# A chunked delta rule feeding an MoE layer: four weight loads wait for ScalarE, and the whole order is written anew

## The chip, the cores and the metric

The kernel runs on one NeuronCore of a Trainium2 chip. The metric is the time of one execution on the device, in microseconds; of several executions the median counts. TensorE (PE) does the matmuls, VectorE (DVE), ScalarE (ACT) and GpSimd (POOL) the work between them, and the sync engine (SP) issues most of the DMAs.

## The reference, cut to what matters

```python
def _attn_ref(q, k, v, beta):               # q, k, v: (4, 8, 768, 48) float32
    k_n = k / (np.linalg.norm(k, axis=-1, keepdims=True) + 1e-06)
    state = np.zeros((B, H, D, D), dtype=np.float32)
    for t in range(S):
        kt, vt, bt = (k_n[:, :, t], v[:, :, t], beta[:, :, t, None])
        y[:, :, t] = np.einsum('bhd,bhde->bhe', q[:, :, t], state)
        v_old = np.einsum('bhde,bhd->bhe', state, kt)
        state = state + bt[:, :, :, None] * np.einsum('bhd,bhe->bhde', kt, vt - v_old)

def _moe_ref(x, w_in, w_out):               # x: y as (3072, 384); w_in (384, 2048), w_out (2048, 384) float64
    h = x @ w_in
    sp = np.where(h > 20.0, h, np.log1p(np.exp(np.minimum(h, 20.0))))
    return (h * np.tanh(sp)) @ w_out
```

A recurrence over 768 steps, for 32 pairs of batch and head, makes y. Every row of y, with the 8 heads side by side, then goes through two matmuls with the Mish function between them.

## The kernel before

**Two halves, woven together.** The 768 steps are cut into 12 chunks of 64 (`NS`). Within a chunk the recurrence is solved as a triangular system; between chunks a 48x48 state is carried. In the program's names, chunk n goes through these stages: `pg` (products of k with k, TensorE) and `d` (masked on DVE); the solve on DVE, an alternation of `pr` and `gt` steps that each need the one before; its result `tu` and `tt`; a merge of the 16-blocks (`ma`, its copy `ym` on ScalarE, `mb`, an addition into `tt` on DVE, then `tn`); `ta` and its copies `at` on ScalarE; `tb` and its copies into `tt`; `pz`; then `py` (the chunk's y) with `ps` (the new state). y is transposed (`xt`) and split into a rounded part and a rest (`x`, ScalarE and DVE). With x the chunk's 256 rows run through the MoE: eight units `g1` (18 matmuls into `h`, then Mish to `e`, its rounded part and its rest `g`) and eight units `g2` (12 matmuls into `acc`). Solves serve two chunks at once, so that of chunks 0 and 1 stands at the very start of the kernel, and no MoE work can start before y of chunk 0 is there.

**The weights.** They come as float64, read as pairs of int32. `load_w` loads 28 tiles: twelve of w_in (`ri0` to `ri11`, 128x1024, two DMAs of 256 KB) and sixteen of w_out (`ro0` to `ro15`, 128x768, two DMAs of 192 KB). The list `parts` numbers them: ri0, ri1, ri2, ro0 to ro3, ri3 to ri5, ro4 to ro7, and so on. `convert` makes float32 of a tile in eight pieces: a clamp on DVE (L1325), a scaling on ScalarE (L1328, or L1331 with one more step on DVE), a shift on DVE (L1338), the join into `mi`, `mo` or `spare` on DVE (L1342), a rounding on ScalarE (L1346), and the rest by two matmuls (`loi`, `loo`, L1354 and L1358) and a copy on ScalarE (L1360), for later tiles by a DMA that adds. The raw tile is overwritten in the end.

**What sets the order.** Every piece of work is a step of a generator that is put on a heap with a number; `run` takes them in the order of the numbers and writes their instructions out, and the scheduler keeps that order on each engine. The numbers stand in a table, `TT`: for each generator the places of its steps, 1612 in all. A second table, `SLOT`, says which buffer a tile takes out of its pool. An instruction waits for the semaphores of what it needs, and everything behind it on its engine waits with it. `warm` matmuls on a tile of zeros are filler on TensorE; they wait for nothing but `zero`.

**DMA queues.** Loads are issued by SP, in the order of their steps; only k's second halves and beta are issued by ScalarE. The loads share eight semaphores in turn, so that a load waits until the eighth before it has landed. `half` is a 128x1 tile that GpSimd writes at the start.

Of the kernel before, what the change touches and what calls it, by code (L numbers as in the profile page):

```python
# [10 lines left out]
F32 = mybir.dt.float32  # L11
# [18 lines left out]
def bcast_in(ap, n):  # L30
# [3 lines left out]

TT = {
    'warm0.501': [0],
    'warm11.602': [1],
    'loadk0': [2],
    'turn_k(0,0)': [3],
    'loadq': [4],  # L40
    'loada': [5],
    'loadk1': [6],
    'warm0.5': [7],
    'turn_k(0,0).0>1': [8],
    'early0': [9, 31, 35, 41, 53, 58, 60, 61, 63, 67, 69, 75, 76, 78, 81, 82, 83, 85, 89, 92, 101, 106, 110, 112, 114, 122, 123, 125, 129, 131, 132, 133, 134, 135, 137, 326, 985],
# [84 lines left out]
    'scale_v(0,1)': [140],  # L130
    'warm12.3': [141],
    'merge0': [144, 146, 164, 166],
    'warm32.2': [147],
    'merge0.0>1': [148],
    'cv6': [151, 177, 199, 243, 246, 255, 259, 308, 703],
    'warm12.003': [153],
    'merge0.1>1': [154],
    'warm11.8': [155],
    'cv7': [158, 183, 214, 222, 240, 297, 313, 364, 1086],
    'loadi6': [159],  # L140
    'loado7': [160],
    'warm0.602': [161],
    'cv9': [163, 188, 231, 258, 269, 277, 289, 295, 992],
    'loadi7': [165],
    'ats_gq[0,1].0>2': [168],
    'merge0.2>1': [169],
    'cv22': [170, 182, 190, 316, 473, 476, 482, 485, 495],
    'warm11.603': [171],
    'warm27.9': [172],
    'warm11.501': [173],  # L150
    'cv17': [174, 210, 337, 402, 418, 420, 440, 441, 755],
    'cv12': [178, 195, 244, 324, 325, 333, 335, 342, 372],
    'merge0.3>1': [179],
    'ats_a[0,1]': [184],
    'warm29.501': [189],
    'cv8': [191, 226, 233, 264, 271, 274, 285, 302, 1000],
    'loado5': [192],
    'cv13': [193, 247, 273, 354, 370, 373, 375, 386, 1334],
    'ats_a[0,0]': [194],
    'cv14': [197, 296, 318, 343, 360, 363, 366, 381, 452],  # L160
    'loado15': [200],
    'ats_a[0,1].0>1': [201],
    'loado13': [202],
    'merge1': [209, 212, 268, 284],
    'ats_a[0,0].0>1': [213],
    'cv15': [215, 219, 221, 350, 358, 362, 371, 380, 1332],
    'loadi8': [218],
    'loadp': [220],
    'merge1.1>1': [223],
    'loadx': [224],  # L170
    'warm46.601': [227],
    'cv11': [228, 249, 251, 283, 286, 320, 332, 338, 881],
    'unit(1,)': [229],
    'warm8.0': [230],
    'cv25': [232, 266, 344, 382, 508, 509, 526, 529, 547],
    'merge1.0>1': [234],
    'ats_b[0,0]': [235],
    'loads': [236],
    'ats_b[0,1]': [238],
    'ats_gq[0,1].0>1': [245],  # L180
    'warm12.301': [248],
    'loadi9': [250],
    'unit(0,)': [252],
    'ats_b[0,0].0>1': [253],
    'ats_b[0,1].0>1': [256],
    'ats_z[0,0]': [257],
    'cv16': [260, 305, 334, 399, 403, 415, 419, 423, 1511],
    'ats_z[0,0].0>1': [261],
    'cv23': [262, 288, 314, 414, 480, 487, 489, 497, 504],
    'ats_z[0,1]': [265],  # L190
    'ats_z[0,1].0>1': [267],
    'merge1.2>1': [270],
    'ats_y[0,0]': [272],
    'ats_y[0,0].0>1': [275],
    'warm12.401': [276],
    'cv21': [278, 322, 330, 396, 435, 446, 461, 462, 472],
    'warm11.801': [279],
    'cv20': [280, 323, 383, 451, 453, 471, 481, 490, 1350],
    'cv27': [281, 351, 374, 530, 548, 551, 561, 566, 578],
    'ats_y[0,1]': [282],  # L200
    'turn_q(1,0)': [287],
    'loadk2': [290],
    'scale_v(1,1)': [291],
    'merge1.3>1': [292],
    'ats_y[0,1].0>1': [293],
    'turn(0,)': [294],
    'turn(0,).0>1': [298],
    'turn_q(1,1)': [299],
    'turn(0,).0>2': [300],
    'turn(0,).0>3': [301],  # L210
    'early1': [303, 353, 355, 368, 384, 390, 395, 400, 401, 404, 407, 408, 413, 416, 422, 424, 427, 428, 432, 433, 434, 445, 450, 455, 458, 460, 463, 464, 475, 478, 479, 484, 491, 494, 500, 505, 507, 510, 512, 513, 515, 518, 520, 527, 531, 532, 533, 537, 539, 540, 543, 544, 545, 546, 553, 557, 559, 560, 563, 568, 571, 572, 574, 575, 576, 577, 580, 584, 586, 588, 602, 613],
    'ats_a[1]': [304],
    'ats_a[1].0>1': [306],
    'scale_v(1,0)': [307],
    'ats_gq[1,0]': [309],
    'turn(0,).0>4': [310],
    'ats_b[1]': [315],
    'ats_gq[1,0].0>1': [317],
    'g1.0.0': [319],
    'ats_b[1].0>1': [327],  # L220
    'ats_gq[1,0].0>2': [328],
    'loadk3': [329],
    'ats_z[1,0]+s_gq[1,1]': [331],
    'warm12.001': [336],
    'ats_z[1,0]+s_gq[1,1].0>3': [339],
    'ats_z[1,0]+s_gq[1,1].0>1': [340],
    'loado14': [346],
    'g1.0.0.0>1': [347],
    'warm42.1': [348],
    'ats_z[1,0]+s_gq[1,1].0>2': [349],  # L230
    'g1.0.0.0>2': [352],
    'g1.0.0.0>3': [356],
    'cv26': [357, 417, 483, 528, 534, 550, 554, 555, 562],
    'ats_y[1,0]': [359],
    'loado12': [361],
    'cv24': [365, 387, 442, 459, 499, 506, 514, 516, 521],
    'g1.0.1': [367],
    'ats_y[1,0].0>1': [369],
    'warm11.701': [376],
    'warm12.2': [377],  # L240
    'g1.0.1.0>1': [378],
    'warm46.6': [379],
    'early1.2>1': [385],
    'early1.3>1': [388],
    'early1.4>1': [389],
    'ats_z[1,1]': [392],
    'g1.0.3': [393],
    'early1.5>1': [394],
    'early2': [397, 502, 585, 589, 493, 590, 600, 609, 616, 622, 625, 626, 628, 632, 634, 643, 644, 651, 655, 663, 664, 665, 675, 676, 678, 679, 680, 681, 682, 684, 685, 688, 690, 691, 692, 693, 694, 695, 700, 707, 708, 709, 711, 712, 715, 716, 719, 725, 727, 728, 733, 738, 739, 740, 742, 744, 745, 746, 747, 749, 752, 753, 757, 758, 760, 761, 764, 768, 770, 771, 777, 786, 798, 817],
    'g1.0.2': [398],  # L250
# [1905 lines left out]
```

## Time and profile before

| | before |
|---|---|
| median of three runs | 636.4 us (632.79 to 640.93) |
| the profiled execution | 633.69 us |
| its span, first to last instruction | 631.9 us |
| mean granted TensorE clock | 0.985 |
| TensorE busy | 605.8 us, 96% |
| DVE busy | 384.2 us, 61% |
| ScalarE busy | 287.2 us, 45% |
| GpSimd busy | 77.8 us, 12% |

A busy share is a mean over stages with different limits, and TensorE's holds filler too. What bounds a stage is read from the chain of waits: from the last instruction back, at each step, to what released it. A time in brackets behind a row of the timeline is the time for which the engine stood before it. The granted clock is a share of full speed.

### The profile page before, as it was taken

The numbers are of one execution on the slowest core, as the hardware profiler recorded it, in microseconds if no ns is written. First come the engines' busy times: TensorE is split into PE (matmuls) and PEld (weight loads), VectorE is DVE, ScalarE is ACT, GpSimd is POOL, SyncE is SP. The second block draws the span as 40 slices with busy tenths as digits, with TensorE's granted clock in tenths as the row PEclk, the third lists the DMA queues.
The fourth block names the chain that finished last, engine by engine and source line by source line (L and its number), as shares of the span: only waits on it lengthen the run. The fifth ranks groups of instructions, "written<-read, shape, count | busy, mean of one in ns | idle before, by whom it ended". The sixth has DMA issues, their size and how long they took to land.

```text
span 631.9 us, 22179 instructions
## 1 busy us (share of the span) xinstructions
PE 605.8 (96%) x9707; PEld 567.1 (90%) x9718; DVE 384.2 (61%) x837; ACT 287.2 (45%) x555; POOL 77.8 (12%) x134
## 2 busy tenths in 40 slices
PE   6888899989999998999999999999999999999997
PEld 4555789889999998999999999999999999999996
DVE  1986678899669899775568567874464321511120
ACT  2356878644543453625444435424432534333141
POOL 5100123323101040020100102210021010000000
PEclk9997989989999999999999999999999999999999
DMA  8996568921433134223223222312212132000011
GB/s 192 278 345 132 89 133 140 147 50 32 71 52 73 27 52 61 50 43 49 47 41 52 52 28 33 65 33 52 33 29 44 28 52 52 1 7 20 1 26 25
DMA packets 161807, 43.21 MB, mean 68 GB/s; under 512 B 149008, under 2 KB 157712, under 8 KB 161712
## 3 DMA queue, kind: packets, MB, share of 16 engines
q1 hardware_dynamic: 156800, 37.12, 29.7%
q0 software_dynamic: 2736, 4.20, 4.0%
q8 instruction: 76, 1.25, 0.8%
q10 hardware_dynamic: 2176, 0.49, 0.4%
q14 instruction: 19, 0.16, 0.1%
HBM read 32.87 MB, written 4.72 MB: 59 GB/s over the span
## 4 chain that ended last, share of the span: by engine, by line
PE 73%; DVE 12%; DMA 5%; SPq 5%; issue 3%; ACT 1%; DVEq 0%
PE acc L1884 27%; PE h L1850 26%; SPq L1266 5%; PE py L1659 3%; PE pz L1659 3%; PE gq L1659 3%; PE pg L1466 3%; DVE gt L1529 2%; DVE pr L1527 2%; PE ps L1659 2%; DVE g L1867 1%; DMA ri<-in_moe_w_in_dram 1%; DMA xx<-in_q_dram 1%; PE warm L1910 1%; DMA kt<-in_k_dram 1%
## 5 line engine op out<-in xcount | busy, mean ns | idle before, releaser
L1884 PE MATMUL acc<-wo,g 128*128 128x384 f32 x1152 | 218.9, 341 | 3.1 <-DVE g L1867 3.1
L1850 PE MATMUL h<-x,wi 128*128 128x256 f32 x1728 | 219.9, 283 | 1.3 <-issue 1.3
L1850 PEld LDWEIGHTS h<-x,wi 128*128 128x128 f32 x1728 | 214.4, 190 | 2.7 <-issue 1.4
L1884 PEld LDWEIGHTS acc<-wo,g 128*128 128x128 f32 x1152 | 198.1, 188 | 5.4 <-DVE g L1867 3.7
L1867 DVE TENSOR_TENSOR g<-e,g 128x512 fp32r<-128x512 f32 x96 | 66.8, 703 | 95.9 <-ACT g L1866 95.5
L1865 ACT ACTIVATE e<-h 128x512 f32<-128x512 f32 x96 | 57.1, 598 | 118.2 <-PE h L1850 81.8
L1866 ACT CAST g<-e 128x512 fp32r<-128x512 f32 x96 | 58.9, 621 | 58.6 <-PE acc L1884 54.8
L1529 DVE TENSOR_TENSOR gt<-gt,pr 128x58 f32<-128x58 f32 (+9 forms) x164 | 60.4, 369 | 4.1
L1527 DVE TENSOR_TENSOR pr<-gt 128x58 f32<-128x58 f32 (+9 forms) x164 | 58.7, 358 | 4.0
L1659 PE MATMUL gq<-xx,kt 48*64 48x112 f32 (+1 forms) x768 | 50.5, 271 | 0.6 <-PE ps L1659 0.4
L1659 PEld LDWEIGHTS pz<-vt,tt 64*64 64x64 f32 x768 | 44.1, 137 | 5.0 <-issue 2.1
L1659 PE MATMUL pz<-vt,tt 64*64 64x48 f32 x768 | 47.8, 227 | 0.8 <-DVE vt L1745 0.8
L1644 DVE STREAM_TRANSPOSE xx<-xx 128x1024 f32<-128x1024 f32 x20 | 24.9, 1244 | 38.8 <-DMA xx<-in_q_dram 30.5
L1659 PEld LDWEIGHTS gq<-xx,kt 48*64 48x64 f32 x768 | 44.8, 133 | 1.9 <-issue 0.8
L1770 ACT COPY xx<-pz 64x384 f32<-64x384 f32 x48 | 22.8, 474 | 41.1 <-PE gq L1659 19.1
L1659 PEld LDWEIGHTS py<-xx 128*64 128x64 f32 x768 | 37.6, 138 | 4.2 <-issue 1.2
L1659 PE MATMUL py<-xx 128*64 128x48 f32 x768 | 41.1, 224 | 0.0
L1748 DVE TENSOR_TENSOR xx<-gq,amask 64x256 f32<-64x256 f32 x96 | 40.2, 418 | 0.9 <-issue 0.2
L1659 PE MATMUL ps<-xx 128*48 128x48 f32 x704 | 37.6, 208 | 0.0
L1637 POOL TENSOR_TENSOR vt<-vt,ne 128x384 f32<-128x384 f32 x24 | 21.2, 891 | 126.6 <-DMA vt<-in_v_dram 126.1
L1568 POOL COPY tt<-d 32x512 f32<-32x512 f32 x40 | 26.5, 663 | 72.3 <-DVE d L1549 49.5
L1659 PEld LDWEIGHTS ps<-xx 128*48 128x48 f32 x704 | 31.4, 125 | 0.0
(138 smaller groups left out, 596.2 us busy)
## 6 DMA issues: line engine op xcount, KB each, us to landing
ri<-in_moe_w_in_dram SPq DMA_DIRECT2D x24, 256.0 KB, 5.2
ro<-in_moe_w_out_dram SPq DMA_DIRECT2D x32, 192.0 KB, 5.1
kt<-in_k_dram SPq DMA_DIRECT2D x76, 64.0 KB, 3.3
vt<-in_v_dram SPq DMA_DIRECT2D x48, 96.0 KB, 3.1
xx<-in_k_dram SPq DMA_DIRECT2D x48, 96.0 KB, 3.2
out_dram<-o SPq DMA_DIRECT2D x48, 96.0 KB, 2.2
xx<-in_q_dram SPq DMA_DIRECT2D x80, 32.0 KB, 2.4
wo<-mo POOLq DMA_DIRECT2D x9, 192.0 KB, 3.9
```

The lines of the kernel that those rows point to most:

```text
L1266: m = (nc.scalar if turns[0] else nc.sync).dma_start(out=dst, in_=src)
L1527: nc.vector.tensor_tensor(out=pv, in0=nj, in1=xj, op=ALU.mult)
L1529: nc.vector.tensor_tensor(out=below, in0=below, in1=pv, op=ALU.add)
L1568: nc.gpsimd.tensor_copy(out=tt2[r, t2, :, c0:c0 + 32], in_=dts[g][r, t2])
L1644: nc.vector.transpose(x, x)
L1659: last[:] = [nc.tensor.matmul(*a, start=True, stop=True)]
L1748: nc.vector.tensor_tensor(out=x[r, p4, hh, D:D + C], in0=ps[r, :, d:], in1=bcast_mid(amask[r], 4), op=ALU.mult)
L1850: nc.tensor.matmul(h[:, f2, :], wt["i", f * P // WI * NCH + c][:, i2, f0:f0 + P], x[:, c, :], start=(i == 0), stop=(i == 3 * NCH - 1))
L1865: for d, f in ((0.7, lambda: nc.scalar.activation(e, h, AF.Mish)), (0.7, lambda: nc.scalar.copy(out=gg[:, 0], in_=e)), (0.8, lambda: nc.ve ...
L1866: (0.7, lambda: nc.scalar.copy(out=gg[:, 0], in_=e)),
L1867: (0.8, lambda: nc.vector.tensor_tensor(out=gg[:, 1], in0=e, in1=gg[:, 0], op=ALU.subtract))):
L1884: nc.tensor.matmul(acc[t], gg[:, a, f2, ts_], wt["o", f][:, i2, :], start=(f == 0 and i == 0), stop=(f == NF - 1 and i == 2))
```

## The change

A new function `gate(k)` makes the raw tile of weight k and lets ScalarE write its first column, a copy of `half`. The load of that tile overwrites the column and so has to wait for the copy. Four weights have a gate, by their places in `parts`: ri0 (0), ro0 (3), ro3 (6) and ro4 (10). The column's value is of no use to anything.

```diff
+GATES = (0, 3, 6, 10)
 TT = {
...
+    'loadk1': [0],
...
+    'gate(0,)': [2],
...
-            r = raw[kind, i] = cp.tile([P, src.shape[1]], I32, tag=f"w{kind}{i}", name=f"r{kind}{i}")
+            if (kind, i) not in raw:
+                raw[kind, i] = cp.tile([P, src.shape[1]], I32, tag=f"w{kind}{i}", name=f"r{kind}{i}")
+            r = raw[kind, i]
...
+    def gate(k):
+
+        kind, i = parts[k]
+        r = raw[kind, i] = cp.tile([P, 1024 if kind == "i" else 2 * DM], I32, tag=f"w{kind}{i}", name=f"r{kind}{i}")
+        nc.scalar.copy(out=r.bitcast(F32)[:, 0:1], in_=half)
+        give(f"gate{k}")
...
-                need=[f"G0{h}{i}" for h in range(2) for i in range(2)] if y == "k3" else ["Y00", "Y01"] if len(todo) < TN['nw'] else ())
+                need=[f"gate{parts.index(y)}"] if isinstance(y, tuple) and parts.index(y) in GATES else [f"G0{h}{i}" for h in range(2) for i in range(2)] if y == "k3" else ["Y00", "Y01"] if len(todo) < TN['nw'] else ())
             i += 1
+    for k in GATES:
+        do(0.2 + k, gate, k)
```

Both tables, TT and SLOT, are new from the first row to the last. No step is lost and none is added but the four gates; the same matmuls, conversions and loads stand in other places, 10 to 30 places away in the first 400, fewer later. Three places matter here.

SP's queue at the start of the program, before (kn0 and kn1 are k of chunks 0 and 1, qn0 is q, vt0 is v; ri and ro are weights):

```order
L1266 DMA kn0_119<-in_k_dram 64x8x48 x2
L1266 DMA qn0_131<-in_q_dram 64x8x48 x4
L1266 DMA kn1_138<-in_k_dram 64x8x48 x2
L1266 DMA ri0_195<-in_moe_w_in_dram 128x512 x2
L1266 DMA ri1_200<-in_moe_w_in_dram 128x512 x2
L1266 DMA ri2_206<-in_moe_w_in_dram 128x512 x2
L1266 DMA ro0_209<-in_moe_w_out_dram 128x384 x2
L1266 DMA ro2_215<-in_moe_w_out_dram 128x384 x2
```

The same queue now, from its first row:

```order
L1271 DMA kn1_115<-in_k_dram 64x8x48 x2
L1271 DMA kn0_127<-in_k_dram 64x8x48 x2
L1271 DMA ri1_133<-in_moe_w_in_dram 128x512 x2
L1271 DMA ri5_136<-in_moe_w_in_dram 128x512 x2
L1271 DMA ri0_123<-in_moe_w_in_dram 128x512 x2
L1271 DMA ri2_207<-in_moe_w_in_dram 128x512 x2
L1271 DMA qn0_217<-in_q_dram 64x8x48 x4
L1271 DMA vt0_0_225<-in_v_dram 64x8x48 x2
L1271 DMA vt0_1_228<-in_v_dram 64x8x48 x2
L1271 DMA ro10_235<-in_moe_w_out_dram 128x384 x2
L1271 DMA ro1_238<-in_moe_w_out_dram 128x384 x2
L1271 DMA ro2_242<-in_moe_w_out_dram 128x384 x2
```

k of chunk 1 has moved to the head of the queue, ahead of k of chunk 0 and of q; q has moved behind four weights, and v up from the 27th to the 15th load. ro0, the seventh row before, is now the fifteenth.

ScalarE's rows now around the third gate, at the end of the solve's preparation (y0 is the norm of k, gt0 and d0 are zeroed, qp0 is the transposed q):

```order
L1504 ACTIVATE y0_379<-y0_379 128x32 [waits Activation_49]
L1506 COPY gt0_375<-zero_76 128x16x16
L1507 COPY d0_171<-zero_76 128x32x16
L1321 COPY ro0_384<-half_89 128x1
L1435 COPY xx0_104<-qp0_0_407 48x8x64 [waits PE_49,Pool_49]
L1435 COPY xx1_105<-qp0_1_420 48x8x64 [waits PE_49,Pool_49]
L1435 COPY xx1_105<-qp0_1_420 48x8x64
L1342 ACTIVATE ro2_242<-ro2_242 128x384 [waits DMAHW7_49,DMAHW6_49,DVE_49]
L1321 COPY ro4_474<-half_89 128x1
```

The two L1321 rows are new: the gates of ro0 and ro4. The scaling of ro2, which waits for its load and for DVE, stands ahead of the second.

TensorE between ta and pz of chunk 0, before:

```order
L1659 MATMUL ta0_0_818<-tt2_108,at0_148 32x32 x16
L1587 MATMUL ma1_0_852<-tu0_587,d0_147 32x16 x32
L1354 MATMUL loo2_888<-spare_111,ident_84 128x384
L1587 MATMUL ma1_1_890<-tu0_587,d0_147 32x16 x32
L1354 MATMUL loo1_930<-mo1_848,ident_84 128x384
L1358 MATMUL loo1_930<-wo1_928,identr_82 128x384
...
L1659 MATMUL tb0_0_962<-at0_148,tn0_586 32x32 x16
L1358 MATMUL loo2_888<-wo2_886,identr_82 128x384
L1659 MATMUL tb0_1_989<-at0_148,tn0_586 32x32 x16
L1354 MATMUL loo0_1010<-mo0_807,ident_84 128x384
```

And now:

```order
L1673 MATMUL ta0_0_820<-tt2_108,at0_172 32x32 x16
L1368 MATMUL loo1_846<-mo1_783,ident_84 128x384
L1601 MATMUL ma1_0_848<-tu0_592,d0_171 32x16 x32
L1673 MATMUL tb0_1_885<-at0_172,tn0_591 32x32 x16
L1372 MATMUL loo1_846<-wo1_844,identr_82 128x384
L1372 MATMUL loo2_814<-wo2_812,identr_82 128x384
...
L1673 MATMUL tb0_0_918<-at0_172,tn0_591 32x32 x16
...
L1673 MATMUL pz0_0_949<-vt0_0_225,tt2_108 64x48 x16
L1601 MATMUL ma1_1_985<-tu0_592,d0_171 32x16 x32
```

The second ma of chunk 1 has moved behind pz, the loo of ro0 and ro3 behind pz as well, and the second half of tb has gone ahead of the first; only four warm matmuls, left out here, stand between the loo and pz around tb0_0.

## Rows read from the trace of the kernel before

**Rows 1.** The page, busy time: us, share of the span, instructions.
```profile
PE 605.8 (96%) x9707; PEld 567.1 (90%) x9718; DVE 384.2 (61%) x837; ACT 287.2 (45%) x555; POOL 77.8 (12%) x134
```
**Rows 2.** Busy time in stretches: stretch, length, engines, clock, DMA share, GB/s.
```profile
core 0: us, PE busy (x) PEld busy (x) DVE busy (x) ACT busy (x) POOL busy (x), PEclk, DMA share, GB/s
37.00:79.30 42.30, 36.35 (x1043) 25.72 (x1047) 29.45 (x70) 29.80 (x65) 5.02 (x7) 0.90 0.70 169
79.30:150.00 70.70, 66.18 (x1031) 62.31 (x1034) 63.12 (x141) 43.58 (x85) 20.16 (x28) 0.94 0.64 108
150.00:627.50 477.50, 473.51 (x7204) 461.74 (x7204) 268.84 (x561) 201.09 (x382) 42.40 (x72) 1.00 0.23 39
```
**Rows 3.** The same view, shorter stretches.
```profile
37.00:50.00 13.00, 11.25 (x420) 7.17 (x421) 11.85 (x30) 9.30 (x21) 1.21 (x2) 1.00 1.04 321
...
55.00:60.00 5.00, 4.78 (x68) 3.31 (x66) 2.06 (x7) 2.70 (x7) 0.00 (x0) 0.50 0.70 131
...
75.00:90.00 15.00, 12.96 (x288) 11.56 (x286) 11.66 (x26) 9.63 (x19) 2.62 (x3) 0.77 0.78 150
```
**Rows 4.** The chain that ended last, 46 to 125 us: start, duration, what.
```profile
50.06 1.94 issue
...
72.26 3.20 DMA kt<-in_k_dram
...
76.75 0.53 DVE x L1826
...
79.27 4.14 PE h L1850 x18
```
**Rows 5.** Timeline of SP's queue: start, duration, line, DMA; xN issues merged.
```profile
0.82 1.67 SPq L1266 DMA_DIRECT2D kn<-in_k_dram  x2
...
6.22 1.31 SPq L1266 DMA_DIRECT2D kn<-in_k_dram  x2
...
21.50 2.64 SPq L1266 DMA_DIRECT2D vt<-in_v_dram  x4
```
**Rows 6.** Timeline of TensorE, chunk 0's stages: start, duration, line, out<-in.
```profile
37.09 1.28 PE L1587 MATMUL ma<-tu,d 16*32 16x16 f32 x128
...
54.73 1.06 PE L1659 MATMUL tb<-at,tn 32*32 32x32 f32 x32
...
60.95 1.13 PE L1659 MATMUL pz<-vt,tt 64*64 64x48 f32 x32
...
64.11 0.32 PE L1659 MATMUL py<-xx 128*64 128x48 f32 x4
```
**Rows 7.** Timeline of DVE, the first solve from d's transposition to tu.
```profile
18.26 1.98 DVE L1481 STREAM_TRANSPOSE gt<-d 128x1024 f32<-128x1024 f32 x1
...
26.94 0.36 DVE L1325 TENSOR_SCALAR ro<-ro 128x384 f32<-128x384 f32 x1
27.21 0.27 DVE L1527 TENSOR_TENSOR pr<-gt 128x112 f32<-128x112 f32 x1
...
32.37 0.86 DVE L1748 TENSOR_TENSOR xx<-gq,amask 64x256 f32<-64x256 f32 x2
...
35.90 1.14 DVE L1540 STREAM_TRANSPOSE tu<-gt 128x512 f32<-128x512 f32 x1
```
**Rows 8.** Timeline of ScalarE: the solve's preparation, and the second at copies.
```profile
20.75 0.23 ACT L1490 ACTIVATE y<-y 128x32 f32<-128x32 f32 x1
...
21.18 0.61 ACT L1493 COPY d<-zero 128x512 f32<-128x512 f32 x1
...
49.52 0.76 ACT L1706 ACTIVATE at<-ta 32x256 f32<-32x256 f32 x2
```
**Rows 9.** Waits of SP, 0 to 80 us: total us, times, longest us.
```profile
SPq L1266 <- PE ps L1659: 7.1, 1, 7.1
```
**Rows 10.** Time to landing: kn's (view of the tile), ro's (the page).
```profile
DMA to landing us min/median/max: 2.8/3.9/4.2
ro<-in_moe_w_out_dram SPq DMA_DIRECT2D x32, 192.0 KB, 5.1
```
**Rows 11.** Timeline of GpSimd: the writing of half.
```profile
1.48 0.22 POOL L1228 MEMSET half<- 32x1 f32 x2
```

More of the change, by code (lines that the diff above doesn't have):

```diff
@@ L167 @@
[L167 to L184, printed above, removed]
@@ new lines @@
+    'turn_k(1,0).0>1': [21],
+    'loadi2': [22],
+    'turn_k(0,1)': [24],
+    'turn_k(0,1).0>1': [25],
+    'loadq': [26],
+    'early0.0>1': [27],
+    'loadv': [28],
+    'warm0.601': [29],
+    'warm12.401': [30],
+    'loado10': [31],
+    'loado1': [32],
+    'turn_k(1,1).0>1': [33],
+    'loado2': [34],
+    'loadi4': [37],
+    'warm11.802': [40],
+    'early0.2>1': [44],
+    'warm12.102': [45],
+    'turn_beta()': [46],
[106 rows of a table added]
+    'loadx': [233],
+    'loads': [235],
+    'cv16': [236, 317, 335, 401, 405, 407, 416, 421, 1583],
@@ L215 @@
+    'turn(0,).0>3': [308],
     'ats_gq[1,0]': [309],
[L216 to L231, printed above, removed]
@@ L451 @@
[L451 to L468 removed]
+    'ats_a[1].0>1': [312],
@@ new lines @@
+    'g1.0.2': [410],
+    'g2.0.0': [413],
+    'ats_z[1,1].0>1': [415],
+    'g1.0.2.0>1': [417],
+    'g1.0.1.0>3': [419],
+    'g1.0.3': [420],
+    'g1.0.2.0>2': [422],
+    'ats_y[1,1]': [424],
+    'g2.0.1': [425],
+    'turn_q(2,0)': [434],
+    'g1.0.4': [435],
+    'g1.0.2.0>3': [442],
+    'g2.0.2': [443],
+    'ats_y[1,1].0>1': [453],
+    'g1.0.3.0>1': [461],
+    'g1.0.3.0>2': [463],
+    'g1.0.4.0>1': [471],
+    'g1.0.4.0>2': [473],
+    'g1.0.3.0>3': [474],
+    'g1.0.5': [475],
@@ new lines @@
+    'g1.0.7.0>2': [547],
+    'g1.0.6.0>1': [548],
+    'g1.0.7.0>3': [549],
+    'scale_v(2,0)': [553],
+    'g2.0.5': [556],
+    'g1.1.0': [560],
+    'g1.0.6.0>2': [562],
+    'g1.0.6.0>3': [570],
+    'ats_gq[2,0].0>2': [572],
+    'g1.1.2.0>1': [573],
+    'g1.1.1': [575],
+    'g2.0.6': [577],
+    'g1.1.2.0>2': [580],
+    'g1.1.2.0>3': [583],
+    'g2.0.7': [589],
+    'g1.1.0.0>1': [591],
+    'g1.1.3': [592],
+    'g2.0.7.0>1': [594],
+    'ats_a[2]': [595],
+    'g1.1.1.0>1': [597],
@@ new lines @@
+    'turn(4,).0>3': [923],
+    'g1.3.5.0>3': [924],
+    'turn(4,).0>1': [925],
+    'turn_q(5,1)': [927],
+    'prep(6,)': [928],
+    'g1.3.7.0>1': [932],
+    'g1.3.6': [933],
+    'turn(4,).0>2': [936],
+    'g1.3.4': [937],
+    'early4.3>1': [938],
+    'g1.3.7.0>2': [940],
+    'g1.3.4.0>1': [942],
+    'turn(4,).0>4': [943],
+    'g1.3.4.0>2': [945],
+    'ats_z[5,0]+s_gq[5,1]+s_a[6]': [946],
+    'g1.3.7.0>3': [948],
+    'g1.3.6.0>1': [949],
+    'g1.3.4.0>3': [950],
+    'g2.3.4': [951],
@@ L826 @@
[L826 to L842 removed]
+    'turn(5,)': [1013],
@@ new lines @@
+    'g1.10.6.0>2': [1559],
+    'g2.10.4': [1560],
+    'g1.10.7': [1561],
+    'g1.10.7.0>1': [1562],
+    'g1.10.7.0>2': [1563],
+    'g2.10.5': [1564],
+    'g1.10.6.0>3': [1565],
+    'turn(11,).0>4': [1566],
+    'g1.11.0': [1567],
+    'g1.11.0.0>1': [1568],
+    'g1.10.7.0>3': [1569],
+    'g1.11.5': [1570],
+    'g1.11.2': [1571],
+    'g1.11.4': [1572],
+    'g1.11.1': [1573],
+    'g1.11.0.0>2': [1574],
+    'g1.11.2.0>1': [1575],
+    'g1.11.2.0>2': [1576],
+    'g1.11.0.0>3': [1577],
```

1663 lines of the change are left out of this document (746 added, 917 removed), and 250 rows, old and new, of tables (SLOT, TT).

## The prediction

> **What bounds the kernel now.** I read the page first: TensorE is busy 605.8 of 631.9 us [rows 1], so only its pauses, its filler and its slow stretches can be won. The busy time by stage says where these are. From 150 us on TensorE pauses 477.5 - 473.5 = 4.0 us at full clock; from 79.3 to 150 it pauses 4.5 us, and at a mean clock of 0.94 it loses about 70.7 x 0.06 = 4.2 us more [rows 2]. Both stretches are bound by TensorE's own work, which the change leaves as it is (the same 3681 rows in its program). The stretch before the first MoE matmul is different: from 37 to 79.3 us TensorE pauses 42.3 - 36.4 = 5.9 us and runs at 0.90 [rows 2], and much of its busy time is filler or work that doesn't set the pace. Here a chain over DVE, TensorE and ScalarE decides, and its end is h at 79.27 us [rows 4]. What the change moves there arrives at the end of the kernel almost one to one, since what follows is TensorE-bound. So I forecast the start of h.
>
> The chain has three legs. First the solve on DVE: it starts with the transposition of d at 18.26 and ends with tu, at 35.90 + 1.14 = 37.04 [rows 7]. Second the stages ma, mb, ta, tb, pz from 37.09 to 60.95 [rows 6]. Third py, xt, the rows x and h, from 64.11 to 79.27 [rows 6, 4]. Two things in it stand out. At 50.06 TensorE stood 1.94 us with nothing named as its releaser [rows 4], at the end of a stretch in which the DMA engines were 1.04 busy, and after it its granted clock was 0.50, the lower of its two levels (1.2 of 2.4 GHz) [rows 3]. And x came only at 76.75, behind DVE's transposition of kt, whose load landed at 72.26 + 3.20 = 75.46; the clock was 0.77 from 75 to 90 [rows 3, 4].
>
> **The gates.** Each adds one 128x1 copy on ScalarE and a semaphore to a load. No 128x1 copy is in the trace. The nearest row is the 128x32 activation of 0.23 us [rows 8]; below, nothing. I take 0.2 us each. ScalarE is busy 29.8 of 42.3 us in its fullest early stretch [rows 2], so 0.8 us hides there; uncovered it would cost 0.8 us. What counts is whether SP has to stand. ri0 is SP's seventh load; the gate needs half, written at 1.48 to 1.70 us [rows 11], and ScalarE's table load, so it is through at about 4, while the load also waits for k0's halves, which land at 7 or later. ro0 is SP's load 29; before, loads 27 to 30 are the four of vt, at 21.50 to 24.14 [rows 5], so SP comes there at about 22.8. Its gate stands right behind the zeroing of d, done before at 21.18 + 0.61 = 21.8 [rows 8], and by the first leg below that comes earlier. ro3's gate is ScalarE's eighth row and ro4's comes some 3 us after ro0's, while those are SP's loads 39 and 43. I expect no gate to hold SP by more than a microsecond; the margin is thinnest at ro0, 1 to 2 us. Behind it stand the other weights, xx, q and vt of chunk 1, and then kt, so whatever holds SP there holds all of them.
>
> A page speaks against such a wait. The Trainium skill (DMA: Bandwidth & Descriptors, Anatomy of one DMA) says that DMA engines don't wait on semaphores and that the issuing sequencer does, before dispatch. The trace agrees: SP stood 7.1 us for one load of xx that needed ps [rows 9], and nothing behind it was issued. By that rule a late gate delays the whole queue; this is the third rival.
>
> **First leg.** Both halves of k now stand at the head of the queue. Before, k1's second half was issued at 6.22, behind q [rows 5]; now SP issues four kn loads from 0.82 at about 0.7 us each, and the last lands at about 3.6 + 4.2 = 7.8 by the longest landing of kn [rows 10]. If ScalarE's half of k0 has to wait for the table load and the gate, it lands at about 9. But ScalarE's second kt copies now stand behind the conversion of ri1, whose load is issued at about 6.5 and lands some 5 us later. So pg ends only a little sooner: I take 0.9 us off the start of the solve (0 to 2.5). In the solve the pair of gq products at 32.37, 0.86 us [rows 7], moves behind tt: -0.87. Conversions between the solve's steps go from five to eight; one occupies 0.36 us [rows 7] and part of that covers the steps' own latency, so +0.15 each, +0.45. One of the eight is the clamp of ro0, just ahead of the step that stood at 27.21 [rows 7] and would now stand at 27.21 - 0.9 + 0.45 = 26.8. ro0's load goes out at 22.8 and 23.5 and takes 5.1 us [rows 10]: 28.6. DVE stands 1.8 us (0 to 2.5). Sum of the leg: -0.9 - 0.87 + 0.45 + 1.8 = +0.5; tu at 37.5 instead of 37.04.
>
> **Second leg.** The second pair of at copies ends at 49.52 + 0.76 = 50.28, 13.2 us after tu [rows 8]. ScalarE has 20 rows from the first ym to there before and 17 now, of the same kinds, so I keep 13.2. Before, tb then started only at 54.73, 4.45 us after its input, because ma, three loo and three filler matmuls stood ahead of it on TensorE with the 1.94 us pause among them. Now nothing of weight stands between at and tb_0: 0.35 us, a gain of 4.1. From tb to pz it took 60.95 - 54.73 = 6.22 us with both tb, three loo pairs and filler between; now tb_1 has gone ahead, and what is left is one tb (0.5), ScalarE's two copies (0.75) and queueing, 2.0: a gain of 4.2. pz to py stays. Together -8.3.
>
> **Third leg.** From py to h it took 79.27 - 64.11 = 15.2 us. TensorE's work between them in the new order (two py stages of 1.8, four loi or loo pairs of 0.8 on average, two mb, xt, ta 1.1, gq 1.75, tb 1.1 and six filler matmuls) is about 14.4 us, and kt's load, which still follows py on SP, would again end x some 13.2 us after py (76.75 + 0.52 - 64.11). So 14.4 governs: -0.8, and the wait on x is covered.
>
> **What I give back.** Legs two and three assume full clock and no pause. The same weights still stream, so a pause of 1.94 us may return, and TensorE now really waits for ScalarE between ta and tb, after which it will probably be granted 0.50 again for about 5 us [rows 3]: +1.9 + 2.5 = +4.4, the whole of it charged. Behind h the 15 us at 0.77 cost 3.4 us; since the wait on x goes I take half back, -1.5. A page differs on the pause: the Trainium skill (Runtime: NRT & Kernel Launch, Instruction fetch mechanics) holds that instruction refills, which run on DMA queues, are mostly hidden. By that page the 1.94 us would not be a refill and need not return, and the time would be 1.9 us less; the row names no cause, and no run here shows one.
>
> **Sum.** +0.5 - 8.3 - 0.8 + 4.4 - 1.5 = -5.7 us. The profiled execution took 633.69 us: 628.0. The median of the three runs is 636.4, 2.7 us more, and I forecast such a median: 630.7, rounded to 631.
>
> **Rivals.**
> *More is kept* (chance 0.22): no pause, no half clock, no wait for ro0, k at its best: -2.5 - 0.4 - 8.3 - 0.8 - 3.4 = -15.4 at the most, 618 to 626 by the median. For it: TensorE's fillers still stand around the waits. Against it: the order before had fillers around its waits too, and still shows the pause and the low clock [rows 3, 4].
> *The gain is eaten* (0.20): the order shortens one queue and lengthens another. Where ta's input comes later on DVE, since the gq pair and two merged weights now stand ahead of mb's additions, 2 to 4 us go, and a second pause takes the rest: -3 to +3, 633 to 640. That the gates do nothing at all belongs to this and to the forecast alike: then only the order speaks.
> *SP stands at a gate* (0.13): ro0's gate, or ro4's, which stands behind the conversion of ro2 and so behind DVE, comes late. DVE then stands in the middle of the solve for ro0, and each microsecond of it moves tu, h and the end. It takes away the forecast gain once ro0 lands 5.7 us after 28.6, at about 34.3, and makes the kernel slower from there on: 640 to 650.
> *Forecast* (0.45): 627 to 634, with the sum above.
>
> **Numbers.** The likeliest time is 631. The range reaches into the neighbours on both sides, 618 to 643; about 0.06 lies below it and 0.09 above. Two per cent of 636.4 is 12.7 us, about what a measurement of this kernel can tell from no change. Under 623.7 lies most of the first rival, 0.18. Over 649.1 lies a part of the third, 0.06. The rest, 0.76, is within.
>
> **What would show it.** The start of h against 79.27 is the test of everything: about 73 to 75 by the forecast, under 70 in the first rival, 78 or more in the second. The solve's tu near 37.5 with a DVE wait of 1 to 2 us on ro0; tb within a microsecond of the at copies; pz less than 3 us behind tb; no wait of SP on ScalarE. I am wrong if h comes early and the end doesn't, which would mean that DVE, 63.1 of 70.7 us busy behind h [rows 2], and not TensorE, sets the pace there; or if new pauses show up behind 150 us, where the order is rewritten as well and I changed nothing.

## The result, and the profile after

The changed kernel takes 628.9 us (median of 16 executions, 623.01 to 636.62) against 635.1 us for the kernel before, run beside it (16 executions, 631.39 to 640.93): a ratio of 0.989, 95% interval 0.985 to 0.992. It is 6 to 7 us faster, which is inside the 2% band. Forecast were 631 us and a time within 2%.

| | after |
|---|---|
| the profiled execution | 625.97 us |
| its span | 624.2 us |
| mean granted TensorE clock | 0.990 |
| start of the first h | 77.99 us (before 79.27) |
| from the first h to the end of the span | 546.2 us (before 552.6) |

The last two rows are the finding. The time was forecast about right, but the gain lies where I did not put it: in these two profiles 1.3 us ahead of the first h and 6.4 us behind it.

The page of after, busy time (answers [rows 1]):

```profile
PE 606.3 (97%) x9718; PEld 561.2 (90%) x9718; DVE 382.1 (61%) x837; ACT 290.9 (47%) x560; POOL 79.2 (13%) x134
```

Busy time in stretches of after, columns as in [rows 2]; the last row is the whole stretch from the first h on:

```profile
37.00:50.00 13.00, 11.27 (x283) 5.81 (x281) 8.24 (x19) 4.65 (x11) 0.00 (x0) 0.87 1.08 302
50.00:60.00 10.00, 8.90 (x300) 5.97 (x298) 7.65 (x20) 7.49 (x18) 1.41 (x2) 1.00 0.57 96
...
75.00:90.00 15.00, 14.87 (x406) 12.71 (x410) 14.32 (x33) 14.65 (x28) 4.05 (x6) 1.00 0.73 124
90.00:150.00 60.00, 57.87 (x939) 54.58 (x929) 54.33 (x125) 37.77 (x76) 19.95 (x28) 1.00 0.61 102
...
77.99:624.20 546.21, 536.33 (x8235) 518.84 (x8233) 328.85 (x702) 247.67 (x468) 63.29 (x99) 1.00 0.29 49
```

The same view of the kernel before, from its first h on:

```profile
79.27:631.90 552.63, 539.72 (x8235) 524.09 (x8236) 331.99 (x701) 245.17 (x466) 62.56 (x99) 0.99 0.29 49
```

Both stretches hold 8235 recorded matmuls, so their sums can be compared: TensorE is busy 3.4 us less (about 1.9 of it the clock, which was 1.00 from 75 to 90 where [rows 3] showed 0.77; e4 below has the old order at full clock) and stands 9.9 instead of 12.9 us. From 37 to 50 the new order is no better than the old: 1.7 us of standing, a clock of 0.87, the DMA engines 1.08 busy.

TensorE in after, timeline (start, duration, what; in brackets how long it stood before the row), from ma to the first h:

```profile
38.77 0.58 PE L1372 MATMUL loi<-wi,identr 128*128 128x512 f32 x1
39.28 1.28 PE L1601 MATMUL ma<-tu,d 16*32 16x16 f32 x128
...
42.33 0.42 PE L1612 MATMUL mb<-tt,ym 32*32 32x16 f32 x26
44.48 0.50 PE L1612 MATMUL mb<-tt,ym 32*32 32x16 f32 x38 [1.73 <-issue]
44.91 2.07 PE L1368 MATMUL loi<-spare,ident 128*128 128x512 f32 x2
...
56.79 0.69 PE L1673 MATMUL tb<-at,tn 32*32 32x32 f32 x32
...
57.99 1.49 PE L1673 MATMUL pz<-vt,tt 64*64 64x48 f32 x32
...
77.99 2.26 PE L1864 MATMUL h<-x,wi 128*128 128x256 f32 x18
```

ma stands behind a filler stretch and a loi until 39.28, though tu was there at 37.26; a pause of 1.73 us with no releaser splits mb after its 26th row; the loi pair behind it takes twice its time.

ScalarE in after, with the first gate and the second pair of at copies:

```profile
2.25 1.28 ACT L1321 ACT_TABLE_LOAD   x1 [2.25 <-issue]
...
3.54 0.19 ACT L1321 COPY ri<-half 128x1 f32<-128x1 f32 x1
...
53.48 0.77 ACT L1720 ACTIVATE at<-ta 32x256 f32<-32x256 f32 x2
```

DVE in after, the wait for ro0 and tu (answers [rows 7]):

```profile
28.89 0.36 DVE L1339 TENSOR_SCALAR ro<-ro 128x384 f32<-128x384 f32 x1 [0.91 <-DMA ro<-in_moe_w_out_dram]
...
36.16 1.10 DVE L1554 STREAM_TRANSPOSE tu<-gt 128x512 f32<-128x512 f32 x1
```

### The profile page after: what moved, and what is told of

Same layout as the page of the kernel before. It is cut to its first block, busy times and chain, and to the rows that moved or that the text cites. A ratio compares the mean times of both kernels' runs of the same rounds, so it can differ in the third digit from the quotient of the medians.

```text
span 624.2 us, 22218 instructions
## 1 busy us (share of the span) xinstructions
PE 606.3 (97%) x9718; PEld 561.2 (90%) x9718; DVE 382.1 (61%) x837; ACT 290.9 (47%) x560; POOL 79.2 (13%) x134
## 3 DMA queue, kind: packets, MB, share of 16 engines
q8 instruction: 77, 1.26, 0.9%
## 4 chain that ended last, share of the span: by engine, by line
PE 75%; DVE 9%; DMA 5%; ACT 4%; issue 3%; SPq 3%; DVEq 0%; ACTq 0%; POOLq 0%
PE acc L1898 27%; PE h L1864 25%; PE warm L1924 4%; PE pg L1480 3%; PE pz L1673 3%; PE py L1673 3%; SPq L1271 3%; PE gq L1673 3%; DVE gt L1543 2%; PE ps L1673 2%; DMA wi<-mi 2%; DVE pr L1541 2%; DMA kt<-in_k_dram 1%; DVE g L1881 1%; PE xt L1836 1%
## 5 line engine op out<-in xcount | busy, mean ns | idle before, releaser
L1864 PEld LDWEIGHTS h<-x,wi 128*128 128x128 f32 x1728 | 211.2, 188 | 3.5 <-issue 1.1
L1543 DVE TENSOR_TENSOR gt<-gt,pr 128x58 f32<-128x58 f32 (+9 forms) x164 | 58.0, 353 | 4.0
L1924 PE MATMUL warm<-zero 128*128 128x512 bf16 x107 | 31.6, 431 | 1.5 <-DVE zero L1220 1.5
```

The lines of the kernel that those rows point to most:

```text
L1543: nc.vector.tensor_tensor(out=below, in0=below, in1=pv, op=ALU.add)
L1864: nc.tensor.matmul(h[:, f2, :], wt["i", f * P // WI * NCH + c][:, i2, f0:f0 + P], x[:, c, :], start=(i == 0), stop=(i == 3 * NCH - 1))
L1924: nc.tensor.matmul(warm, zb[:, 0:P], zb[:, :512], start=True, stop=True)
```

## The experiments

Each was timed in turns with the kernel before, and each left one profile. The length of the pauses ahead of h varies from execution to execution of one kernel (the profiled ones of e1, e2 and e3 are among the longest of their kernels), so single profiles are compared only by where something stands, and by the stretch behind h.

| kernel | ratio to before, 95% | first h | h to end |
|---|---|---|---|
| before (profile of before) | 1 | 79.27 | 552.6 |
| after (profile of after) | 0.989 [0.985, 0.992] | 77.99 | 546.2 |
| e1 after again | 0.988 [0.983, 0.994] | 85.58 | 547.3 |
| e2 after, no gates | 0.987 [0.982, 0.993] | 85.13 | 546.5 |
| e3 after, 8 fillers fewer | 0.982 [0.978, 0.986] | 86.53 | 545.7 |
| e4 before, wait filled | 0.998 [0.995, 1.001] | 74.62 | 552.0 |
| e5 after, loads held | 0.998 [0.995, 1.001] | 84.42 | 545.5 |
| e6 after, fillers split | 0.994 [0.990, 0.997] | 78.19 | 553.9 |
| e7 fewer and split | 0.999 [0.996, 1.003] | 76.26 | 555.5 |
| e8 before, scaling later | 0.996 [0.993, 0.999] | 77.92 | 551.5 |
| e9 after, scaling back | 0.985 [0.980, 0.990] | 77.52 | 546.9 |
| e10 fewer, split, 128 more | 0.988 [0.984, 0.992] | 78.19 | 546.9 |
| e11 fewer, loads held | 0.991 [0.987, 0.994] | 81.98 | 546.5 |
| e12 as e3, another chip | 0.982 [0.977, 0.986] | 76.43 | 548.4 |

The last column is the span less the start of the first h. The old order needs 551.5 to 552.6 us there, the new one 545.5 to 548.4, whether h came at 76 or at 86; e6 and e7, at 554 and 555, are told below. Ahead of h the two orders overlap.

**The changed kernel again, and without the gates.**

> The changed kernel itself, as the yardstick for the next two. 7 us under the kernel before (0.989). Two theories share it. ORDER: the gain comes from the new order alone, and most of it lies behind the first h, where the clock no longer falls. GATES: the four gates steer the DMA queue and carry a part of it.

```diff
-GATES = (0, 3, 6, 10)
+GATES = ()
```

> The new order with the four gate copies and their waits taken out. ORDER: the same time as the changed kernel within 1 us, since no row of the trace shows SP waiting for ScalarE; ScalarE loses four copies of 0.19 us and one table load of 1.28 us near 3.8 us, all of which lay in idle time; ro0 is issued at 22.4 as before. GATES: ro0 and the loads behind it come out earlier, the DMA engines are fuller at the start of the solve, and the time moves by 2 us or more, either way.

629.1 us with the gates and 629.9 us without, 0.988 and 0.987. The gates do nothing to the time that can be measured; without them the order alone is as fast.

**Eight fillers fewer ahead of ma.**

```diff
-              warm=[..., (11.703,2), ..., (11.803,2), ..., (27.9,2), ..., (43.6,2), ...],
+              warm=[..., (11.703,0), ..., (11.803,0), ..., (27.9,0), ..., (43.6,0), ...],
```

> The new order with 8 of the filler matmuls that stand between the solve's last gq and the first ma taken out (they ran at about 0.21 us each, and ma started 2.0 us after tu). FILLER theory: ma starts at once behind tu, at 37.5 to 38.0 instead of 39.28, h at 76.5 to 77.3 instead of 77.99, the end 0.7 to 1.5 us earlier. Rival, kt: x waits for kt's load, which follows SP's queue and not TensorE, so h stays at 78 and the end too. Rival, CLOCK: TensorE stands and its clock falls, 1 to 3 us slower. For the pauses without a releaser: if they belong to a place in the program (the 128th matmul from the last one), the pause inside mb now comes after 34 of its rows instead of 26, and the one in ta after 23 instead of 15; if they belong to a time or to a kind of work, they stay after 26 and 15 rows or move at random.

> The kernel with 8 fillers fewer once more, on another chip, since it was the fastest so far and its interval (0.9777 to 0.9858) touches that of the changed kernel (0.9828 to 0.9939). FILLER theory: ma stands behind tu and not behind fillers, which is worth 0.7 to 1.5 us, and the ratio to the kernel before is 0.980 to 0.987. Rival, CHANCE: the difference lay in how long the pause in mb happened to be, and the ratio is 0.988 or more. By the trace: the pause in mb after its 34th row again, the stretch from the first h to the end 545 to 547.

TensorE in the second of these runs, timeline:

```profile
37.54 1.29 PE L1601 MATMUL ma<-tu,d 16*32 16x16 f32 x128 [1.30 <-DVE tu L1554]
...
41.35 0.48 PE L1612 MATMUL mb<-tt,ym 32*32 32x16 f32 x34
43.97 0.43 PE L1612 MATMUL mb<-tt,ym 32*32 32x16 f32 x30 [2.14 <-issue]
```

ma now waits for tu and not for fillers. Both runs give 0.982, about 4 us less than the changed kernel. It is the fastest version found, clearly faster than the kernel before; against the changed kernel the intervals still overlap a little. That 4 us are more than the 0.7 to 1.5 expected stays unexplained. The fastest executions are hardly faster (622.4 and 625.2 us, against 623.0 of after), so it may lie in how often the long ones come. The pause moved exactly as its place in the program demands: eight matmuls fewer ahead of it, eight rows further into mb (34 instead of 26). Its length did not shrink: 2.42 us in e3, which with the low clock behind it put h at 86.53, and 2.14 us in e12, where h came at 76.43.

**Where the pauses stand.** A count of TensorE's matmuls up to each pause, by the view of busy time with stretches that start at 0, first in the kernel before, then in after:

```profile
0.00:42.11 42.11, 33.73 (x597) 19.88 (x602) 27.78 (x78) 15.68 (x33) 10.21 (x28) 1.00 0.92 265
0.00:46.49 46.49, 37.52 (x723) 22.29 (x730) 31.09 (x88) 18.53 (x38) 11.42 (x30) 1.00 0.92 269
0.00:51.98 51.98, 41.08 (x851) 24.55 (x857) 35.08 (x98) 22.89 (x48) 11.42 (x30) 1.00 0.92 261
```

```profile
0.00:44.46 44.46, 38.36 (x601) 20.97 (x602) 27.03 (x76) 17.62 (x37) 10.19 (x28) 0.92 0.94 274
0.00:51.20 51.20, 44.60 (x728) 23.94 (x729) 31.34 (x88) 20.75 (x44) 11.20 (x30) 0.90 0.94 264
0.00:55.31 55.31, 48.22 (x856) 26.27 (x856) 35.39 (x99) 24.68 (x52) 11.60 (x30) 0.91 0.92 252
```

The weight loads (second count; a few matmul records are missing) say 602, 730, 857 and 602, 729, 856: the same places, 127 or 128 apart, under different work. In the same moment a packet of the queue named instruction is on the wire. DMA queues of after from 42.0 to 43.2 us (packets, MB, share of the 16 engines):

```profile
q1 hardware_dynamic: 323, 0.44, 100.3%
q8 instruction: 1, 0.02, 4.9%
```

Over the whole kernel that queue moved 77 packets and 1.26 MB, which is 16 KB each, one for about every 126 of 9718 matmuls and as many weight loads. So the next 16 KB of TensorE's program are asked for as it goes, get in line behind the weights, and TensorE stands if 128 matmuls are through before they land. The starts of these packets in the traces bear this out. In the two runs told next in which the DMA engines are empty here, e5 and e11, the packet starts 0.8 to 0.9 us after TensorE has passed the boundary before; in the others it starts 1.2 us (e4, no pause) to 3.9 us (e3, a pause of 2.42) after it. Wherever TensorE stood at this boundary, it went on 2.2 to 2.6 us after the packet's start. The Trainium skill (Runtime: NRT & Kernel Launch, Instruction fetch mechanics) says that the program is fetched in blocks of 16 KiB, 256 instructions, and that crossing a boundary is mostly hidden. The block agrees with these counts; "hidden" doesn't hold here for small matmuls under full DMA engines, while behind h, with the engines 0.29 busy, the blocks of after cost 0.9 us together. At this boundary after stood 1.73 us; over the other executions with full engines it was 0.7 to 2.6 us, and in one, e4, nothing.

**Is it the weights that the refill waits for?** ro4's gate was moved behind the second ym copy, and three loads behind it:

```diff
-    'gate(10,)': [95],
+    'gate(10,)': [171.2],
...
-    'loadi6': [137],
+    'loadi6': [171.31],
...
-    'loado4': [150],
+    'loado4': [171.30],
...
-    'loado5': [168],
+    'loado5': [171.32],
```

> The new order, with the gate of ro4 moved behind the second ym copy of ScalarE and with the loads of ro4, ri6 and ro5, and all behind them, moved behind that gate: SP stands from about 36 to 43 us and the DMA engines run empty by about 41. REFILL theory: TensorE's pause in mb (1.73 us in one profile, 2.64 in another, always after its 26th row) is a wait for the next 16 KB of the program, which come as a packet of the instruction queue and get in line behind the weights; with the engines empty the packet starts sooner and the pause is at most 0.5 us, and the clock from 37 to 60 is 1.00. Rival, PLACE: the pause belongs to this place whatever the DMA engines do, and stays at 1.5 us or more. The time as a whole decides nothing here, because the weights come 7 us later: 622 to 640.

Busy time with the loads held, then TensorE's timeline:

```profile
37.00:43.00 6.00, 4.76 (x200) 2.91 (x201) 5.61 (x11) 1.94 (x4) 0.00 (x0) 1.00 0.02 5
```

```profile
41.37 0.73 PE L1612 MATMUL mb<-tt,ym 32*32 32x16 f32 x64
...
44.19 0.73 PE L1612 MATMUL mb<-tt,ym 32*32 32x16 f32 x64
...
55.90 0.32 PE L1673 MATMUL tb<-at,tn 32*32 32x32 f32 x4 [5.94 <-ACT at L1720]
```

With the DMA engines at 0.02 from 37 to 43 us, where after has 1.04, mb runs through without a pause, the clock stays at 1.00 up to 52, and ta is through by 48.5 instead of 53.1. This is the refill, shown by taking its competitor away. The late weights then cost more than was won: DVE and ScalarE stood for ri7 until 53.7, with the at copies behind them, and the clock fell to 0.58 from 52 to 60. That is the forecast's third rival, brought about here by moving the gate. In a second try ri7 was loaded ahead of the hold, with eight fillers fewer:

```diff
-    'loadi7': [185],
+    'loadi7': [137],
```

> Fewer fillers, and the loads held behind the second ym copy as before, but with ri7, for whose clamp DVE and ScalarE then stood until 53.7, loaded ahead of the hold. REFILL theory: no pause over 0.5 us from 37 to 46, ta through by about 48, at within 2 us of it, no wait of TensorE for at over 1 us, h at 73 to 78 in the profile, and the ratio 0.975 to 0.982. Rival, LATE WEIGHTS: another weight is waited for in its place (DVE or ScalarE stands 3 us or more between 48 and 65 for ri6, ri11 or ro4), h at 80 or later, ratio 0.99 or more.

Busy time, and TensorE's timeline:

```profile
38.00:43.00 5.00, 4.33 (x175) 2.28 (x164) 4.38 (x9) 1.89 (x4) 0.00 (x0) 0.76 0.02 3
49.00:54.10 5.10, 2.90 (x121) 1.89 (x121) 4.03 (x11) 3.84 (x9) 0.32 (x1) 1.00 1.01 347
```

```profile
51.38 0.47 PE L1673 MATMUL tb<-at,tn 32*32 32x32 f32 x19
54.05 0.43 PE L1673 MATMUL tb<-at,tn 32*32 32x32 f32 x13 [2.20 <-issue]
```

No pause up to 51, and then 2.20 us at the boundary in tb, once the held loads fill the engines again. That boundary cost 0.27 us after the same row in e12. The bytes have to come some time; holding them moves the pause. The numbers are those of LATE WEIGHTS (h at 81.98, ratio 0.991, DVE standing 6.76 us for a w_in load until 61.29), but neither theory foresaw this pause, and from 56 to 82 us TensorE names no weight that it waited for; the clock behind the pause is 0.52 from 54 to 60.

**Moving the boundaries.** In e6 and e7 the fillers between the last gq and ma were written as more and narrower matmuls; in e10, 68 narrow ones were added near 5 us to e7. In e6 (e7 has `6 * n` of 64 columns in place of `4 * n` of 128, and the eight fillers out):

```diff
-        for _ in range(n):
-            nc.tensor.matmul(warm, zb[:, 0:P], zb[:, :512], start=True, stop=True)
+        m, cols = (4 * n, 128) if 125 < now[0] < 159 else (n, 512)
+        for _ in range(m):
+            nc.tensor.matmul(warm[:, :cols], zb[:, 0:P], zb[:, :cols], start=True, stop=True)
```

> The new order, with the 20 filler matmuls between the last gq and ma written as 80 of a quarter of the width: the same filling, 60 matmuls more in the program. REFILL theory: the boundary now lies after row 100 of ma instead of row 26 of mb, and the one before it among the fillers, so that the next 16 KB are asked for near 36 instead of 39.6 and have come when they are needed; the next boundary lies after row 22 of the second mb. No pause of more than 0.5 us between 36 and 50, h at 75 to 77, the median 2 to 5 us under that of the changed kernel. Rival, MOVES: the pause stays 1.7 us or more and only moves, to row 100 of ma, and the time stays at 629 or is longer, because the split fillers take longer.

> The new order with 8 of the 20 fillers taken out, as in the run with fewer fillers, and the other 12 written as 72 of an eighth of the width: 52 matmuls more than in the changed kernel. REFILL theory: as with the split fillers, the boundary lies in ma, here after row 108, and in the second mb after row 30; no pause over 0.5 us between 36 and 50, ma starts within 0.3 us of tu, the median at 621 to 624, and all executions under 628, where those with fewer fillers alone reached 634.7. Rival, MOVES: the pause is as long at its new place, and some executions still take 630 or more.

> The kernel with fewer and split fillers, with 68 narrow matmuls more near 5 us, where TensorE waits for k anyway: 128 more in all than the kernel with fewer fillers. PHASE theory: the program comes to TensorE in blocks of 128 matmuls, so all boundaries lie where they lie with fewer fillers alone: the pause in mb is back after its 34th row, the pauses without a releaser behind the first h sum to 1.5 to 2 us (they were 7.6 with 52 to 60 more, 1.5 with fewer fillers), the stretch from h to the end is 545 to 547 instead of 555.5, and the ratio to the kernel before 0.98 to 0.985. Rival, NARROW: the narrow fillers themselves cost the time, and it stays at 0.997 to 1.0 and 555.

TensorE's waits behind the first h (releaser: sum, times, longest), in e6:

```profile
PE pg L1480 <- issue: 5.0, 6, 1.1
PE h L1864 <- issue: 1.9, 1, 1.9
PE gq L1673 <- issue: 1.9, 3, 0.9
```

The same in e10:

```profile
PE gq L1673 <- issue: 0.8, 1, 0.8
...
PE pg L1480 <- issue: 0.4, 1, 0.4
PE warm L1925 <- issue: 0.3, 2, 0.2
```

Ahead of h my theory failed. The pause went to row 101 of ma (row 100 was expected) and was 2.19 us long there. The boundary before was indeed passed near 36, at 35.86, but the packet started only at 38.29 and ma was at row 101 by 38.69: narrow fillers let 128 matmuls pass as fast as small work does, and what hides a refill is time between two boundaries, not an early request. Behind h these runs showed more than I had asked for. 60 matmuls more, and every later boundary falls on other work: pauses without a releaser sum to 9.1 us in e6 instead of 1.7 in after (0.9 at h, 0.8 at gq), and the stretch takes 553.9 us in e6 and 555.5 in e7. In e6 7.5 of the 9.1 us follow a packet of the instruction queue by 2 to 3 us. The 0.8 at gq do not: they stand at one place in all profiles of the new order, with no such packet within 4 us before their end, so not every pause without a releaser is a refill. With 128 more than e3 the stretch is back at 546.9 us, and the pause at row 34 of mb. The ratio is not back as far as expected: 0.988 (0.984 to 0.992), where 0.98 to 0.985 was expected. Narrow fillers are not to blame for the stretch; the phase of the program against its blocks is, at 7 to 10 us in these profiles.

**The clock behind h.** The kernel before, with fillers where TensorE had stood 1.88 us for x:

```diff
+    'warm75.0': [314.5],
-               warm=[..., (46.601,1)],
+               warm=[..., (46.601,1),(75.0,6)],
```

> The kernel before, with six filler matmuls ahead of the tb that waits from 75.54 to 77.42 for x. CLOCK theory: the clock of 0.51 from 77.4 to 83.5 comes from standing idle there; filled, it stays at 1.00, h x18 takes 2.3 us instead of 4.2, and the kernel gains 1 to 3 us on the kernel before (0.995 to 0.998) though the wait for x is as long as it was and six matmuls have been added. Rival: the low clock comes from something else (the full DMA engines, the heavy stretch before), stays at about 0.5, and the time is the same or 0 to 1 us longer.

Busy time, and the row of the first h:

```profile
75.00:90.00 15.00, 14.13 (x382) 11.42 (x380) 13.13 (x32) 12.17 (x24) 3.40 (x5) 1.00 0.71 140
```

```profile
74.62 2.53 PE L1851 MATMUL h<-x,wi 128*128 128x256 f32 x18
```

The clock is 1.00 and h takes 2.53 instead of 4.14 us [rows 4]. But in this execution the pause in ma was 0.61 instead of 1.94 us and x was not waited for, so what the fillers did can't be told from it. What it does tell: at full clock the stretch from h to the end still takes 552.0 us. TensorE is busy 1.9 us less than in the profile of before and stands 1.3 us more. The ratio, 0.998, is no measurable gain. So the clock from 75 to 90, which I had charged with 3.4 us, does not by itself make the gain of the new order behind h: this one profile has it at 1.00 and needs as long as before.

**GpSimd beside the second solve.** In the kernel before, two scalings of v on GpSimd stand inside DVE's second solve, near 129 and 135; in the new order one does. DVE of before, then GpSimd, and TensorE's wait from 130 to 140:

```profile
134.17 1.82 DVE L1529 TENSOR_TENSOR gt<-gt,pr 128x198 f32<-128x198 f32 x1
```

```profile
134.62 1.14 POOL L1637 TENSOR_TENSOR vt<-vt,ne 128x384 f32<-128x384 f32 x1
```

```profile
PE acc L1884 <- DVE g L1867: 2.6, 1, 2.6
```

The gt step before it took 0.38 us. One scaling was moved out in the old order, and back in the new one:

```diff
-    'scale_v(2,1)': [556],
+    'scale_v(2,1)': [616.5],
```

> The kernel before, with one of the two GpSimd scalings of v of chunk 2 (near 129.0, inside DVE's second solve) moved behind that solve, to the place which the new order gives it. PORT theory: a DVE step of the solve that runs beside such a scaling takes 1.7 to 1.8 us instead of 0.36, so one of the two slow gt steps goes, TensorE's wait for g near 135 shrinks from 2.55 to about 1.2 us, and the stretch from the first h to the end shrinks from 552.0 to 552.6 (two profiles of this order) to 550 to 551. Ratio to the kernel before 0.997. Rival: the solve is hidden there, the wait for g moves elsewhere, and the stretch stays at 552 to 553.

```diff
-    'scale_v(2,1)': [622],
+    'scale_v(2,1)': [561.5],
```

> The new order, with the second GpSimd scaling of v of chunk 2 moved back into the second solve, as in the order before. PORT theory: a second slow gt step of 1.4 to 1.8 us appears, TensorE waits 1 to 2 us more near 130 to 140, and the stretch from the first h to the end grows from 545.5 to 547.3 (five profiles of this order) to 547.5 to 549; ratio to the kernel before 0.990 to 0.993. Rival: it stays at 546, since DVE has room in the new order.

The wait in e8, then DVE's step in e9:

```profile
PE acc L1884 <- DVE g L1867: 1.2, 1, 1.2
```

```profile
126.36 2.47 DVE L1543 TENSOR_TENSOR gt<-gt,pr 128x220 f32<-128x220 f32 x1
```

In the old order the wait shrinks from 2.55 to 1.20 us, as expected, the stretch behind h by 0.5 to 1.1 us, and the kernel gains 0.4% (0.993 to 0.999). Putting it back into the new order costs nothing that can be measured (0.985): both scalings, back to back, there delay the same gt step, 2.47 instead of 1.70 us. So this is about one of the six microseconds. In e8 the scaling that stayed, at 132.19, delays a join of ro in place of a gt step: 1.91 us, where the join of ro at 132.06 in before took 0.55. The Trainium skill (Trainium Architecture — The Big Picture, What this means for kernel authors) says that DVE and GpSimd share a pair of ports under an exclusive lock; the step of 1.82 us beside a scaling of 1.14 agrees.

More of the six can be read from the profiles, though no run takes it apart. TensorE's waits for g behind the first h, in before and then in after:

```profile
PE acc L1884 <- DVE g L1867: 3.1, 2, 2.6
```

```profile
PE acc L1898 <- DVE g L1881: 0.2, 1, 0.2
```

They sum to 3.1, 3.0 (e4) and 2.3 us (e8) in the old order, and to 0.9 or less in all eleven profiles of the new one.

## Why the prediction was right, and where it was not

The number, 631 against 628.9, was right by luck, out of errors that cancel: up to h I forecast -4.2 us and the profile of after has -1.3, behind h -1.5 and it has -6.4. By its own test, the start of h, the forecast was wrong: 73 to 75 was forecast, 77.99 came, and 78 or more was to speak for "the gain is eaten".

- **The gates: right.** 0.19 us each, hidden; SP never stood for ScalarE; without them no difference can be measured. Not foreseen was that the first gate brings a table load of its own, 1.28 us, hidden as well.
- **First leg: right.** The wait for ro0 was 0.91 us (forecast 1.8, range 0 to 2.5), tu came at 37.26 (37.5). The solve started at 17.61 (forecast 17.4), though a pause of 1.69 us with no releaser stood in pg ahead of it.
- **Second leg: wrong, by a missing term.** 17 rows on ScalarE "of the same kinds, so I keep 13.2" was the step that failed. The copies ended at 54.25, 17.0 us after tu. ma came 2.0 us after tu because TensorE was still at its fillers, which the old order had not shown, and the pause stood in mb, ahead of the copies, not in ma behind them. One half of tb then followed the copies by 0.25 us, at 54.50; the other, for which 0.35 was forecast, by 2.5, since the first half, a pause of 0.49 us in it and a loo pair stood ahead. pz followed that by 1.2 us (forecast 2.0). From tu to pz it took 20.7 us instead of 23.9: -3.2, where legs and give-back together said about -3.9. "pz to py stays" failed too: 4.3 us instead of 3.2, +1.1.
- **Third leg: -0.8 forecast, +0.5 measured.** py to h took 15.7 us; TensorE stood 0.76 us for x.
- **What I give back: right in kind.** A pause came again, 1.73 us, with half clock behind it (0.55 from 45 to 48.7). But it is not the one that I charged: it stands at the first of the three boundaries, where before stood 0.92 us, and the 1.94 us at the third became 0.49. All three sum to 2.7 us, in before to 3.3. And I had charged a pause as something that may return. Its place is fixed by the program; its length is what differs between executions.
- **Behind h: mis-sized, -1.5 against -6.4.** That this part is "bound by TensorE's own work, which the change leaves as it is" was the step that failed. The work is the same, but its order is rewritten there too, and the order decides on what work the blocks' boundaries fall and when TensorE asks DVE for g. Shown by a run is about 1 us for the scaling (e8). By the two profiles TensorE waits 2.9 us less for g, which holds that one, and stands 1.1 us less with no releaser (2.8 us behind h in before, 1.7 in after; of these, 1.3 and 0.9 us follow an instruction packet). Which rows of the new order bring the rest, most of the 6 us, is not isolated: no run took them apart.

How far the pause's length carries is seen in e1, the same program as after. There it was 2.64 us, and the two stretches behind it read, in the view of busy time:

```profile
50.00:60.00 10.00, 10.00 (x176) 5.78 (x171) 7.36 (x19) 5.38 (x12) 1.41 (x2) 0.50 0.65 116
60.00:75.00 15.00, 15.00 (x307) 10.55 (x307) 5.55 (x13) 9.60 (x22) 0.00 (x0) 0.64 0.16 41
```

h then came at 85.58 instead of 77.99. A start of h read from one profile of each kernel, on which the whole forecast rested, is uncertain by more than the 4 to 6 us that were forecast for it.

Of the rivals, "SP stands at a gate" did not occur, and "more is kept" neither. "The gain is eaten" describes the part ahead of h. The last sentence had named the rewritten order behind h as a danger; it was the gain. One bound is mis-added: -15.4 us from the median of 636.4 is 621, and 618 only from the profiled execution.

## What to carry to other kernels

When a table rewrites the whole order, compare the stretches in which both kernels do the same work, count for count, before explaining the one place that looks interesting; one long stretch with few pauses can hold more than the visible stall. A pause of TensorE that names no releaser, stands at the same count of matmuls in two programs and ends 2 to 3 us behind the start of a packet of the instruction queue was a refill here; without such a packet, as at gq, it was not. Look how many small matmuls run between two boundaries while loads fill the DMA engines, and expect any matmul added early to move all boundaries behind it. And take several profiles before a forecast is hung on a stall whose length varies.

## What was not expected of the hardware

- TensorE's pauses lie 127 or 128 matmuls apart in its program, at 602, 729 or 730, and 856 or 857 weight loads, whatever the order, and move to the row when matmuls are taken out (34 for 26, eight fewer) or added.
- At one and the same boundary TensorE stood 0 to 2.6 us with the DMA engines 0.96 to 1.06 busy, and not at all at 0.02. The packet of the next block started 1.2 to 3.9 us behind the boundary before in the one case, and 0.8 to 0.9 us in the other.
- 60 extra matmuls near 36 us made the 546 us behind the first h 7 to 10 us longer; 128 did not.
